# Attention and FFN mix on one core: first keys in halves, first queries in two banks, the end in two halves, and new numbers for the planner

## The chip, the cores and the metric

The kernel runs on one core of one Trainium2 chip. The metric is the device time of one execution in microseconds (us), lower is better. Before the change it is 751.2 us, the median of three runs (751.11 to 751.69).

The core has five engines that run unsynchronised, each with its own queue of instructions, all issued in the program's order: TensorE (PE) for matrix products, ScalarE (ACT), VectorE (DVE), GpSimd (POOL) and SyncE (SP, which here only issues DMAs). TensorE writes to PSUM, which has eight banks of 512 fp32 columns on 128 partitions.

## The reference

The input is 2048 rows x of 512 columns. Its output mixes a 32-head attention block (head width 16) and a SwiGLU FFN (width 1792) by a gate for each row:

```python
g = _sigmoid((x * gate_w).sum(-1, keepdims=True))
a = _A_ref(x, A_wqkv, A_wo)          # softmax(q k^T / 4) v, then @ wo
b = _B_ref(x, B_w_gate, B_w_up, B_w_down)   # (silu(x@wg) * (x@wu)) @ w_down
return g * a + (1 - g) * b
```

All tensors are bf16. The costly part is the softmax: 32 heads x 2048 x 2048 exponentials.

## The kernel before

**Tiling.** The 32 heads form 8 groups of 4; the 2048 queries form 4 blocks of 512. A *unit* is one group with one block of queries (32 units). Each unit has 16 *tiles* of 128 keys; a tile is four score banks, one for each head, of 128 keys x 512 queries. There are 512 tiles; the code counts them as slots. For each tile TensorE makes the scores (keys as weights, queries streamed, in row tiles of the array: mode "R"), an engine takes the exponential from PSUM, and TensorE multiplies the result with the values (`pv`, four matmuls in column tiles of the array: mode "C"), summing into a bank `o` for the unit. A column of ones among the values gives the softmax's denominators.

**Two ways to the exponential.** ScalarE takes most tiles, two banks at a time (1024 columns, `e_all`). VectorE takes the rest, from the last tiles of each unit: it writes scaled bits of the score as an integer (`c_t`, first one bank after another), then either three shifted copies, of which GpSimd can make some (a group of 4 terms), or two bit masks and a product (a group of 2 terms); each term is one more `pv` on TensorE.

**The planner.** Nothing of this order is fixed by loops. While the program is being written, a loop (L1986 on) keeps a model of each engine's clock (`plan.pe`, `plan.act`, `plan.dve`, `plan.pool`) and of when each bank comes free, and chooses the next thing for TensorE: a group of scores (`choose`, L874, and `emit_group`, L982), a `pv`, or a piece of side work from a list of chains with due times (`Pacer`, L50; `side`, L1880): projections of q, k and v, the FFN, output projections. `spend` (L419) charges TensorE's time: `FLIP` for a change of mode, `UNIT_US` or `PIECE_US + COLS_US` for a unit of four matmuls. `horizon` (L863) says when ScalarE will run dry by `ACT_FIX + ACT_COL` a bank, and the scores are put no later than `LATEST` ahead of that (L2004). Whether a tile goes to VectorE is decided by `wants` and `v_unit` (L1940) from VectorE's planned backlog. Some 26 weights steer the choices; `begin` (L1844) sets them anew at the slots that the table `WEIGHTS` (L160) names, some every 8 slots. So a number of the planner changes no arithmetic but can change the order of everything behind it.

**Banks.** `ordered` (L223) gives each instruction that touches a PSUM bank a wait on the last user of that bank if that was another engine, readers included. Two engines can't read one bank side by side.

**The start** (L1574 to L1612). Warm-up matmuls run while x arrives. Chunks 3 and 2 of the transposed input `xT` are made by TensorE from rows of x (`turn`) and copied out by ScalarE and VectorE; chunks 0 and 1 come by two transposing DMAs issued from SP. Then 8 matmuls give the keys of the first head group for 1024 keys (`kp0`, two banks; for each chunk in the order 3, 0, 2, 1, both banks), 4 more the queries of the first block (`qp0`, one bank). VectorE takes the largest absolute key of each row over all 1024 columns (`largest`), scales a selector by it (`k_neg`), and TensorE adds, with |q| that ScalarE made (`aq0`), a bound to the queries (`bound_add`): it keeps the exponent negative. From the bounded queries VectorE makes variant 0 (heads 0 and 2) and then, the bank being the same, ScalarE variant 1 (heads 1 and 3) of `q0a`. Then the planner's loop begins.

**The end.** The last unit's sums are made ready for division in `post` (L1426) by one ScalarE instruction over 512 queries (`osb`); `denominators` (L1482) picks out the sums, `recip16` inverts, `spread_rows` (L1486) spreads them over the partitions, four VectorE products make `on_l`, and four matmuls add the last group's share to four banks `a_ps`, which hold the output projection of the last 512 rows. The rest of that projection is 20 steps: 3 chunks `wo_t`, one `wo_l`, one that adds the FFN part, for each of four banks of 128 rows. Two banks are made as a side chain in halves of the rows (`two_banks`, L541; `last_pieces`, L1501; ten steps of two matmuls), the other two by `tail(n)` (L1517) as full-array matmuls: `tail(3)` ahead of the last two `pv` (L2055), `tail(2)` ahead of the denominators, `tail(2)` ahead of `spread_rows`, three after it.

Of the kernel before, what the change touches and what calls it, by code (L numbers as in the profile page):

```python
# [81 lines left out]
def kernel(  # L82
# [35 lines left out]
    EB = 9  # L118
    NE = 22
    NP = 8  # L120
    NY = 3
# [12 lines left out]
    HUNGRY = 0.107  # L134
    KEEP = 2
    FED = 8.063
    W3 = -1
    N1 = 6
    N2 = 0.964
    LOW = 0.782  # L140
    EXTRA = 1.717
    NEXT = 1.088
    BURST = 8.876
    SHORT = 15
    BACK = 3
    FIRST = 0.087
    W3T = 0.28
    W4 = 0.5
    W4T = 0.168
    W4B = 0.126  # L150
    LATEST = 0.64
# [3 lines left out]
    SPARE = 0.352  # L155
# [109 lines left out]
    class Ordered:  # L265
# [4 lines left out]
        def __getattr__(self, name):  # L270
            f = getattr(self.engine, name)

            def g(*a, **kw):
                out = kw["out"] if "out" in kw else a[0] if a else None
                return ordered(f(*a, **kw), [v for v in (*a, *kw.values()) if v is not out], [out])  # L275
            return g
# [129 lines left out]

    FLIP, UNIT_US, PIECE_US, COLS_US = 0.097, 0.224, 0.011, 0.213
    TO_ACT, ACT_FIX, ACT_COL, ACT_IN = 0.485, 0.064, 0.4265, 0.167
    ACT_PE, DVE_PE, PE_DVE, ACT_DVE = 0.055, 0.08, 0.24, 0.06
    GPS = 1  # L410
    OWN = 1
# [4 lines left out]
    GLEAD = 5.422  # L416
    WINDOW = 1.303

    def spend(mode, mms, ready=0.0):  # L419

        plan.seq += 1
        work_at.append((plan.pe, mms))
        plan.pe = max(plan.pe + (FLIP if mode != plan.mode else 0.0), ready) + (0.226 * mms if mode == "F" else PIECE_US + COLS_US * mms)
        plan.mode = mode
# [52 lines left out]
    def m_tile(name):  # L477
        return take(m_bank())
# [88 lines left out]
    def columns(n, name, lhs, rhs, end, c0=0):  # L567

        st = {}

        def pc(k):
            def f():
                if k == 0:
                    st["p"] = m_tile(name)
                w, r = lhs(k), rhs(k)
                for j in range(4):
                    mm(st["p"][32 * j:32 * j + 32, c0:QBW], lhsT=w[:, 32 * j:32 * j + 32], rhs=r, start=(k == 0),
                       stop=(k == n - 1), tile_position=(0, 32 * j), skip_group_check=True)
# [30 lines left out]
    def v0(t0):  # L609

        p = m_tile("vp")
        for i in range(8):
            for dc in range(DC):
                mm(p[:, 64 * i:64 * i + 64], lhsT=xT[:, dc, (t0 + i) * P:(t0 + i + 1) * P], rhs=wv[:, dc, 0:64],
                   start=(dc == 0), stop=(dc == DC - 1))
        return p
# [865 lines left out]
    def denominators(p, osb):  # L1482
        for tq in range(TQ):
            mm(p[:, 4 * tq:4 * tq + 4], lhsT=osb[:, tq * P:(tq + 1) * P], rhs=sel_t[:, :], start=True, stop=True)

    def spread_rows(p, rt):  # L1486
        for tq in range(TQ):
# [6 lines left out]
    a_ps = []  # L1494
# [6 lines left out]
    def last_pieces():  # L1501

        def keep(pa, pb):
            a_ps.extend([pa, pb])
        return two_banks(NB + 1, "a_l", last_rows(0), last_rows(1), keep, stop=False)

    rest = [(tq, i) for tq in (2, 3) for i in range(NB + 1)]

    def tail_ready():
        for c in sorted(pace.chains, key=lambda c: c.deadline):  # L1510
            force(c)
        while owed:
            pay()
        assert here_done and len(scaled) == TQ
        a_ps.append(m_tile("al"))

    def tail(n):  # L1517

        for _ in range(n):
            tq, i = rest.pop(0)  # L1520
            if tq == 3 and i == 0:
                a_ps.append(m_tile("al_o"))
            w, r = last_rows(tq)(i)
            mm(a_ps[tq][:, 0:D], lhsT=w, rhs=r, start=(i == 0), stop=False)
# [25 lines left out]
    kpart0 = const.tile([P, 3], F32, name="kpart0")  # L1550
# [41 lines left out]
    largest(0, kp0[:, :])  # L1592
    k_neg(kneg1, 0, idle[:, 0:P])
    act(out=aq0, in_=qp0[:, :], func=ACT.Abs)
    act(out=kaug[:, 0, 0:2 * QBW], in_=kp0[:, :], func=ACT.Identity, bias=onescol[:, 0:1], scale=1.0)
    vp0 = v0(0)
    bound_add(qp0, kneg1, aq0)
    vec.tensor_scalar(out=q0a[:, 0, :], in0=qp0[:, :], scalar1=vsel[:, 0:1], scalar2=None, op0=ALU.mult)
    act(out=q0a[:, 1, :], in_=qp0[:, :], func=ACT.Identity, scale=vsel[:, 1:2])
    vec.tensor_copy(out=v0_out(0), in_=vp0[:, :].rearrange("p (t h c) -> p t h c", h=4, c=DH))  # L1600
    m_free(vp0, 0.0)
    vec.tensor_copy(out=q0_bf[0], in_=qp0[:, :])
    m_free(qp0, plan.pe + 2.0)
    m_free(warm, 0.0)
# [118 lines left out]
    for pos, qb in enumerate(ORDER):  # L1723
# [13 lines left out]
        for tq in range(TQ):  # L1737
# [19 lines left out]

# [282 lines left out]
    while closed < UNITS or vops or vcur or jobs:  # L2040
# [89 lines left out]
```

## Time and profile before

One execution was profiled, 751.17 us in all; the span of its instructions is 749.4 us.

| | value |
|---|---|
| median of three runs | 751.2 us (751.11 to 751.69) |
| profiled execution | 751.17 us |
| its span, first to last instruction | 749.4 us |
| granted TensorE clock | 1.00 |
| ScalarE exponentials | 754 of 1024 columns, 4 of 1536 |
| VectorE first steps of a tile from PSUM (banks) | 528, that is 132 tiles of 512 |
| GpSimd busy | 246.2 us (33%) |
| chain that ended last, by engine | ACT 70%, PE 24%, DVE 4%, issue 2% |

In lists of groups each line names the source line, engine, operation, what is written from what, the count, then the busy time and mean ns of one, then the idle time before them and who ended it. Every operation is recorded by a helper (L260 for matmuls, L263 for ScalarE, L275 for the others), so groups are told apart by tiles. In a timeline a line begins with the start and length in us; in a table of stretches each engine has its busy time with the number of instructions in brackets. Engines work in a pipeline, so lengths of neighbours can overlap.

### The profile page before, as it was taken

To read this page: it belongs to the slowest core of one execution; us is meant where nothing else is said; L and a number is where in the kernel's file an instruction comes from. 1 tells how busy PE (TensorE), PEld (TensorE's weight loads), DVE (VectorE), ACT (ScalarE), POOL (GpSimd) and SP (SyncE) were. 2 spreads that over 40 slices of the span, in tenths; PEclk is the share of its full clock that TensorE was granted. 3 is DMA by queue.
4 is the path that set the end of the run, shared out by engine and by line. 5 is a ranking of instruction groups with operands and counts; after the bars stand their busy time and mean duration, and the time that the engine had idled before them with its cause. 6 is when DMAs were issued, how large, how long until landed. Compare 5 with 4: busy or idle time off the path is not lost.

```text
span 749.4 us, 23683 instructions
## 1 busy us (share of the span) xinstructions
PE 733.1 (98%) x10009; PEld 237.0 (32%) x10009; DVE 724.2 (97%) x1196; ACT 733.5 (98%) x827; POOL 246.2 (33%) x342
## 2 busy tenths in 40 slices
PE   7999999999999999999999999999999999999997
PEld 3333332333332333333333233233333333332332
DVE  6799999999999999999999999999999999999995
ACT  5999999999999999999999999999999999999996
POOL 5142030442534443531443322553113403403221
PEclk9999999999999999999999999999999999999999
DMA  9000212344210003220200041312000231200001
GB/s 211 23 2 16 51 32 42 72 121 101 49 36 13 20 24 82 58 53 21 59 16 11 25 109 31 70 27 60 18 23 16 62 82 42 47 19 14 14 31 36
DMA packets 91025, 34.48 MB, mean 46 GB/s; under 512 B 75488, under 2 KB 90472, under 8 KB 90920
## 3 DMA queue, kind: packets, MB, share of 16 engines
q1 hardware_dynamic: 89192, 32.66, 18.5%
q8 instruction: 78, 1.28, 0.7%
q10 hardware_dynamic: 1728, 0.33, 0.3%
q14 instruction: 27, 0.22, 0.1%
HBM read 21.55 MB, written 2.35 MB: 32 GB/s over the span
## 4 chain that ended last, share of the span: by engine, by line
ACT 70%; PE 24%; DVE 4%; issue 2%; DVEq 0%
ACT e_all L263 66%; PE psum L260 24%; ACT th L263 3%; DVE c_t L275 2%; DVE mt L275 0%; DVE gs L275 0%; DVE kaug L275 0%; ACT mt L263 0%; ACT xT L263 0%; DVE rd L275 0%; ACT osb L263 0%; DVE osb L275 0%; DVE o_t L275 0%; DVE qx L275 0%; DVE rn L275 0%
## 5 line engine op out<-in xcount | busy, mean ns | idle before, releaser
L263 ACT ACTIVATE e_all<-psum 128x1024 bf16<-128x1024 f32 x758 | 709.7, 1126 | 1.2 <-PE psum L260 1.0
L275 DVE TENSOR_SCALAR c_t<-psum 128x512 uint16<-128x512 f32 x443 | 295.4, 686 | 4.4 <-PE psum L260 3.3
L260 PE MATMUL psum<-qx,kaug 32*128 32x512 bf16 (+1 forms) x1632 | 250.3, 385 | 6.0 <-ACT e_all L263 4.4
L275 POOL TENSOR_TENSOR c_t<-c_t,lift 128x256 int32<-128x256 int32 (+2 forms) x152 | 105.7, 702 | 274.5 <-DVE c_t L275 216.3
L260 PE MATMUL psum<-e_all,vaug 128*32 128x512 bf16 (+3 forms) x2032 | 169.5, 330 | 0.0
L260 PEld LDWEIGHTS <-kaug 32*128 32x128 bf16 (+1 forms) x2048 | 76.3, 91 | 268.8 <-ACT e_all L263 195.7
L260 PEld LDWEIGHTS <-vaug 128*32 128x32 bf16 x4012 | 96.8, 95 | 125.1 <-issue 88.4
L260 PE MATMUL psum<-c_t,vaug 128*32 128x512 bf16 (+3 forms) x1712 | 132.9, 337 | 0.5 <-DVE mt L275 0.2
L275 DVE TENSOR_SCALAR c_t<-c_t 128x2048 uint16<-128x2048 uint16 (+1 forms) x191 | 129.8, 686 | 0.9
L275 POOL TENSOR_TENSOR c_t<-c_t 128x512 bf16<-128x512 bf16 (+2 forms) x54 | 49.7, 933 | 84.8 <-DVE c_t L275 45.8
L260 PE MATMUL psum<-wd_t,mt 128*32 128x512 bf16 x896 | 73.4, 382 | 0.0
L260 PE MATMUL psum<-xT,wg 128*32 128x512 bf16 x896 | 72.6, 384 | 0.0
L260 PE MATMUL psum<-xT,wu 128*32 128x512 bf16 x896 | 71.7, 383 | 0.4 <-DVE c_t L275 0.3
L275 DVE TENSOR_TENSOR c_t<-c_t 128x2048 bf16<-128x2048 bf16 (+1 forms) x42 | 50.9, 1213 | 0.0
L260 PE MATMUL psum<-q,kaug 32*128 32x512 bf16 (+1 forms) x256 | 50.1, 385 | 0.5 <-ACT e_all L263 0.2
L275 DVE TENSOR_SCALAR kaug<-psum 128x512 uint16<-128x512 f32 (+1 forms) x67 | 44.8, 687 | 0.8 <-PE psum L260 0.4
L260 PE MATMUL psum<-xT,wqk 128*32 128x512 bf16 x512 | 40.9, 383 | 0.0
L263 ACT ACTIVATE th<-psum 128x512 bf16<-128x512 f32 x56 | 38.8, 693 | 0.0
L275 DVE SCALAR_TENSOR_TENSOR gs<-th,psum 128x512 bf16<-128x512 bf16 x56 | 37.9, 676 | 0.4 <-ACT th L263 0.3
L275 DVE SCALAR_TENSOR_TENSOR mt<-gs,psum 128x512 bf16<-128x512 bf16 x56 | 37.9, 677 | 0.3
L275 POOL TENSOR_TENSOR kaug<-c_t,lift 128x256 int32<-128x256 int32 (+1 forms) x31 | 21.1, 681 | 50.3 <-DVE c_t L275 33.2
L275 POOL TENSOR_TENSOR c_t<-kaug,lift 128x256 int32<-128x256 int32 (+1 forms) x30 | 20.7, 697 | 40.1 <-DVE c_t L275 19.7
(124 smaller groups left out, 464.0 us busy)
## 6 DMA issues: line engine op xcount, KB each, us to landing
wg<-in_B_w_gate_dram SPq DMA_DIRECT2D x56, 128.0 KB
wu<-in_B_w_up_dram SPq DMA_DIRECT2D x56, 128.0 KB
on<-osb SPq DMA_DIRECT2D x120, 16.0 KB
rb<-rr SPq DMA_DIRECT2D x15, 128.0 KB
wd_t<-in_B_w_down_dram SPq DMA_DIRECT2D x7, 256.0 KB
qx<-qst SPq DMA_DIRECT2D x96, 16.0 KB
qx<-aq SPq DMA_DIRECT2D x96, 16.0 KB
out_dram<-o_t SPq DMA_DIRECT2D x12, 128.0 KB
```

The costliest lines, as they stand in the source:

```text
L260: return ordered(nc.tensor.matmul(out, lhsT=lhsT, rhs=rhs, **kw), [lhsT, rhs], [out])
L263: ordered(nc.scalar.activation(out=out, in_=in_, **kw), [in_, *kw.values()], [out])
L275: return ordered(f(*a, **kw), [v for v in (*a, *kw.values()) if v is not out], [out])
```

## The change

Four parts.

1. *First keys in halves, first queries in two banks.* The key matmuls run bank by bank, not chunk by chunk. `largest`, `k_neg` and the copy to `kaug` run for each half of 512 keys. The queries are made in two halves of 256, one in bank 4, the other in bank 7 (`warm`, which held the warm-up); |q|, the bound and the variants are made for each half, variants of one half by VectorE, of the other by ScalarE. Three of the eight value tiles go ahead of the bound, five behind.
2. *End in two halves of the queries.* `osb` is made by two ScalarE instructions of 256 queries; denominators, reciprocal, spreading and `on_l` run by halves. The 20 steps become four side chains of five steps in column tiles (mode "C"), released 8, 6, 4 and 2 slots ahead of the end; `tail(n)` takes what is left of them. `tail(3)` ahead of the last `pv` is gone; up to five steps lie between the denominators' parts and the rest ahead of the third final matmul.
3. *Planner.* Durations: `FLIP` 0.097 to 0.1055, a unit 0.224 to 0.2157, a new `TURN` of 0.0105 on entering mode "C", `ACT_FIX` 0.064 to 0.057. All first weights and nearly all entries of `WEIGHTS` are new (55 entries of 26 numbers become 54 of 27; `LATEST` is now among them). Averaged over slots 8 to 511 by the tables: the bound on the exponentials waiting for `pv` (`EB`) 9.2 to 8.6, the share of slots in which VectorE does GpSimd's kind of work itself (`OWN`) 0.86 to 0.62, `LATEST` 0.640 to 0.657.
4. The wrapper of VectorE's and GpSimd's calls records a tensor as read also where it is the output (in-place operations).

```diff
-    FLIP, UNIT_US, PIECE_US, COLS_US = 0.097, 0.224, 0.011, 0.213
-    TO_ACT, ACT_FIX, ACT_COL, ACT_IN = 0.485, 0.064, 0.4265, 0.167
+    FLIP, UNIT_US, PIECE_US, COLS_US, TURN = 0.1055, 0.2157, 0.0024, 0.2133, 0.0105
+    TO_ACT, ACT_FIX, ACT_COL, ACT_IN = 0.485, 0.057, 0.4265, 0.167
...
-        plan.pe = max(plan.pe + (FLIP if mode != plan.mode else 0.0), ready) + (0.226 * mms if mode == "F" else PIECE_US + COLS_US * mms)
+        plan.pe = max(plan.pe + (FLIP if mode != plan.mode else 0.0), ready) + (TURN if mode == "C" != plan.mode else 0.0) + (0.226 * mms if mode == "F" else PIECE_US + COLS_US * mms)
...
-            act(out=osbs[un][:, :], in_=o[:, :], func=ACT.Identity, bias=tiny[:, 0:1], scale=1.0)
+            for cs in (slice(0, QBW // 2), slice(QBW // 2, QBW)):
+                act(out=osbs[un][:, cs], in_=o[:, cs], func=ACT.Identity, bias=tiny[:, 0:1], scale=1.0)
...
-        return two_banks(NB + 1, "a_l", last_rows(0), last_rows(1), keep, stop=False)
+        return columns(NB + 1, "al", lambda i: last_rows(tq)(i)[0], lambda i: last_rows(tq)(i)[1], keep, stop=False)
...
-    for dc in arrived:
-        for tb in range(2):
+    for tb in range(2):
+        for dc in arrived:
             mm(kp0[:, tb * QBW:(tb + 1) * QBW], lhsT=wpad[1][:, dc, :], rhs=xT[:, dc, tb * QBW:(tb + 1) * QBW],
...
-    for dc in arrived:
-        mm(qp0[:, :], lhsT=wpad[0][:, dc, :], rhs=xT[:, dc, 0:QBW], start=(dc == arrived[0]), stop=(dc == arrived[-1]))
-    largest(0, kp0[:, :])
+    HW = QBW // 2
+    halves = [(qp0[:, 0:HW], slice(0, HW)), (warm[:, 0:HW], slice(HW, QBW))]
+    for p, cs in halves:
+        for dc in arrived:
+            mm(p, lhsT=wpad[0][:, dc, :], rhs=xT[:, dc, cs], start=(dc == arrived[0]), stop=(dc == arrived[-1]))
+    largest(0, kp0[:, 0:QBW])
     k_neg(kneg1, 0, idle[:, 0:P])
...
+    largest(3, kp0[:, QBW:2 * QBW])
+    k_neg(kneg1, 3, kneg1)
+    act(out=kaug[:, 0, 0:QBW], in_=kp0[:, 0:QBW], func=ACT.Identity, bias=onescol[:, 0:1], scale=1.0)
+    for p, cs in halves:
+        act(out=aq0[:, cs], in_=p, func=ACT.Abs)
+    act(out=kaug[:, 0, QBW:2 * QBW], in_=kp0[:, QBW:2 * QBW], func=ACT.Identity, bias=onescol[:, 0:1], scale=1.0)
+    vp0 = m_tile("vp")
+    v0(vp0, range(3))
+    for p, cs in halves:
+        bound_add(p, kneg1, aq0[:, cs])
+    v0(vp0, range(3, 8))
+    for v in range(2):
+        vec.tensor_scalar(out=q0a[:, v, halves[0][1]], in0=halves[0][0], scalar1=vsel[:, v:v + 1], scalar2=None, op0=ALU.mult)
+        act(out=q0a[:, v, halves[1][1]], in_=halves[1][0], func=ACT.Identity, scale=vsel[:, v:v + 1])
...
-    pace.add(last_pieces(), SLOTS - KT // 2, SLOTS, downs, cond=ripe)
+    for tq in range(TQ):
+        last.append(pace.add(last_pieces(tq), SLOTS - (KT // 2, 6, 4, 2)[tq], SLOTS + tq, downs, cond=ripe, begun=last[-1:]))
...
-        if closed == UNITS - 1 and pv_left(closed) <= 2 and not a_ps[2:]:
-            tail_ready()
-            tail(3)
         next_pv()
...
+    tail(3)
     on_l = work.tile([P, QBW], BF16, tag="rd", name="on_l")
+    rts = []
+    for h in range(2):
+        dt = m_tile("dt")
+        denominators(dt, osb, (2 * h, 2 * h + 1))
+        rts.append(work.tile([P, 4 * TQ], BF16, tag="rt", name="rt"))
+        recip16(rts[h][:, 8 * h:8 * h + 8], dt[:, 8 * h:8 * h + 8])
+    tail(1)
+    for h in range(2):
+        rps = m_tile("rps")
+        spread_rows(rps, rts[h], (2 * h, 2 * h + 1))
+        for tq in (2 * h, 2 * h + 1):
+            cs = slice(tq * P, (tq + 1) * P)
+            vec.tensor_tensor(out=on_l[:, cs], in0=osb[:, cs], in1=rps[:, cs], op=ALU.mult)
+    tail(1)
+    while len(a_ps) < 2:
+        tail(1)
     for tq in range(TQ):
+        if tq == 2:
+            tail(TQ * (NB + 1))
         mm(a_ps[tq][:, 0:D], lhsT=on_l[:, tq * P:(tq + 1) * P], rhs=wo_l[:, 1, :], start=False, stop=True,
```

More of the change, by code (lines that the diff above doesn't have):

```diff
@@ L117 @@
     UNIT = [(qb, 0) for qb in range(QB)] + [(qb, g) for qb in range(QB) for g in range(1, G)]
-    EB = 9
+    EB = 10
     NE = 22
@@ L133 @@
     D_US = (0.0, 0.6, 1.133)
-    HUNGRY = 0.107
+    HUNGRY = 0.208
     KEEP = 2
-    FED = 8.063
-    W3 = -1
+    FED = 7.822
+    W3 = -0.842
     N1 = 6
[L139 to L142, printed above, removed]
+    N2 = 2.473
+    LOW = 1.544
+    EXTRA = 1.184
+    NEXT = 1.047
     BURST = 8.876
[L144 to L151, printed above, removed]
+    SHORT = 12
+    BACK = 2
+    FIRST = 0.245
+    W3T = -0.164
+    W4 = 4
+    W4T = 0.255
+    W4B = 0.186
+    LATEST = 0.599
     TINY = 1e-37
@@ L274, in g @@
                 out = kw["out"] if "out" in kw else a[0] if a else None
-                return ordered(f(*a, **kw), [v for v in (*a, *kw.values()) if v is not out], [out])
+                reads = [*a["out" not in kw:], *(v for k, v in kw.items() if k != "out")]
+                return ordered(f(*a, **kw), reads, [out])
             return g
@@ L405 @@
     held = [None] * NP
-    FLIP, UNIT_US, PIECE_US, COLS_US = 0.097, 0.224, 0.011, 0.213
-    TO_ACT, ACT_FIX, ACT_COL, ACT_IN = 0.485, 0.064, 0.4265, 0.167
+    FLIP, UNIT_US, PIECE_US, COLS_US, TURN = 0.1055, 0.2157, 0.0024, 0.2133, 0.0105
+    TO_ACT, ACT_FIX, ACT_COL, ACT_IN = 0.485, 0.057, 0.4265, 0.167
     ACT_PE, DVE_PE, PE_DVE, ACT_DVE = 0.055, 0.08, 0.24, 0.06
     GPS = 1
-    OWN = 1
+    OWN = 0
     POOL_IN, POOL_FIX, POOL_ONE, POOL_PE, POOL_OVER = 0.12, 0.12, 0.43, 0.2, 0.1
@@ L415 @@
     TAKE_C = 1
-    GLEAD = 5.422
-    WINDOW = 1.303
+    GLEAD = 5.764
+    WINDOW = 1.503
     def spend(mode, mms, ready=0.0):
@@ L565, in two_banks, with columns @@
         return [(1, pc(k), 2 if k == 0 else 0, "R", st if k == n else None) for k in range(2 * n)]
-    def columns(n, name, lhs, rhs, end, c0=0):
+    def columns(n, name, lhs, rhs, end, c0=0, stop=True):
         st = {}
@@ L577, in f @@
                     mm(st["p"][32 * j:32 * j + 32, c0:QBW], lhsT=w[:, 32 * j:32 * j + 32], rhs=r, start=(k == 0),
-                       stop=(k == n - 1), tile_position=(0, 32 * j), skip_group_check=True)
+                       stop=(stop and k == n - 1), tile_position=(0, 32 * j), skip_group_check=True)
                 spend("C", 1)
@@ L607, in k_bound, with v0 @@
         vec.tensor_reduce(out=kb[:, b:b + 1], in_=kst[b][:, :], axis=AX.X, op=ALU.max, apply_absolute_value=True)
-    def v0(t0):
-        p = m_tile("vp")
-        for i in range(8):
+    def v0(p, tiles):
+        for i in tiles:
             for dc in range(DC):
-                mm(p[:, 64 * i:64 * i + 64], lhsT=xT[:, dc, (t0 + i) * P:(t0 + i + 1) * P], rhs=wv[:, dc, 0:64],
+                mm(p[:, 64 * i:64 * i + 64], lhsT=xT[:, dc, i * P:(i + 1) * P], rhs=wv[:, dc, 0:64],
                    start=(dc == 0), stop=(dc == DC - 1))
-        return p
     def v0_out(t0):
@@ L1480, in recip, with denominators, spread_rows @@
             at.setdefault(n0 + 13 + b, []).append(lambda norm=norm: later(0.345, norm, fast=True))
-    def denominators(p, osb):
-        for tq in range(TQ):
+    def denominators(p, osb, tqs=range(TQ)):
+        for tq in tqs:
             mm(p[:, 4 * tq:4 * tq + 4], lhsT=osb[:, tq * P:(tq + 1) * P], rhs=sel_t[:, :], start=True, stop=True)
-    def spread_rows(p, rt):
-        for tq in range(TQ):
+    def spread_rows(p, rt, tqs=range(TQ)):
+        for tq in tqs:
             for j in range(4):
@@ L1493 @@
     here_done = []
-    a_ps = []
+    a_ps = {}
     def last_rows(t):
@@ L1499, in last_rows, with last_pieces, keep @@
                           (osbs[UNITS - 2][:, cs], wo_l[:, 0, :]) if i == NB - 1 else (ident[:, :], bblk[:, t, :]))
-    def last_pieces():
-        def keep(pa, pb):
-            a_ps.extend([pa, pb])
-        return two_banks(NB + 1, "a_l", last_rows(0), last_rows(1), keep, stop=False)
[L1507 to L1515, printed above, removed]
+    def last_pieces(tq):
+        def keep(p):
+            a_ps[tq] = p
+        return columns(NB + 1, "al", lambda i: last_rows(tq)(i)[0], lambda i: last_rows(tq)(i)[1], keep, stop=False)
+    last = []
     def tail(n):
         for _ in range(n):
[L1520 to L1524, printed above, removed]
+            c = next((c for c in last if not c.out()), None)
+            if c is None:
+                return
+            while not ripe():
+                if owed:
+                    pay()
+                else:
+                    for f in at.pop(min(at)):
+                        f()
+            emit_piece(c)
     def out_pieces(qb, tq):
@@ L1548, in keep_warm @@
             mm(warm[:, :], lhsT=idle[:, 0:P], rhs=idle[:, :], start=True, stop=True)
-    kpart0 = const.tile([P, 3], F32, name="kpart0")
+    kpart0 = const.tile([P, 4], F32, name="kpart0")
     kneg0 = mt[:, 3, P:2 * P]
@@ L1594 @@
[L1594 to L1599, printed above, removed]
-    vec.tensor_copy(out=v0_out(0), in_=vp0[:, :].rearrange("p (t h c) -> p t h c", h=4, c=DH))
-    m_free(vp0, 0.0)
@@ L1602 @@
-    vec.tensor_copy(out=q0_bf[0], in_=qp0[:, :])
-    m_free(qp0, plan.pe + 2.0)
-    m_free(warm, 0.0)
+    HW = QBW // 2
[4 more added lines that the diff above has]
+    largest(0, kp0[:, 0:QBW])
+    k_neg(kneg1, 0, idle[:, 0:P])
+    largest(3, kp0[:, QBW:2 * QBW])
+    k_neg(kneg1, 3, kneg1)
@@ L1605 @@
+    vec.tensor_copy(out=v0_out(0), in_=vp0[:, :].rearrange("p (t h c) -> p t h c", h=4, c=DH))
+    for p, cs in halves:
+        vec.tensor_copy(out=q0_bf[0][:, cs], in_=p)
+    m_free(vp0, plan.pe + 1.0)
+    m_free(qp0, plan.pe + 1.6)
+    m_free(warm, plan.pe + 2.0)
     for g in (3, 4):
@@ L1844, in begin @@
     def begin(n):
-        nonlocal HUNGRY, KEEP, FED, W3, W3T, W4, W4T, W4B, N1, N2, LOW, EXTRA, NEXT, SPARE, BURST, SHORT, BACK, FIRST, EB, OWN, NY, TAKE_C, TAKE_P, GLEAD, WINDOW, FACE
+        nonlocal HUNGRY, KEEP, FED, W3, W3T, W4, W4T, W4B, N1, N2, LOW, EXTRA, NEXT, SPARE, BURST, SHORT, BACK, FIRST, EB, OWN, NY, TAKE_C, TAKE_P, GLEAD, WINDOW, FACE, LATEST
         plan.slot = n
         if n in WEIGHTS:
-            HUNGRY, KEEP, FED, W3, W3T, W4, W4T, W4B, N1, N2, LOW, EXTRA, NEXT, SPARE, BURST, SHORT, BACK, FIRST, EB, OWN, NY, TAKE_C, TAKE_P, GLEAD, WINDOW, FACE = WEIGHTS[n]
+            HUNGRY, KEEP, FED, W3, W3T, W4, W4T, W4B, N1, N2, LOW, EXTRA, NEXT, SPARE, BURST, SHORT, BACK, FIRST, EB, OWN, NY, TAKE_C, TAKE_P, GLEAD, WINDOW, FACE, LATEST = WEIGHTS[n]
         for c in need.get(n, []):
@@ L2006 @@
             n_pv = pv_list(plan.pe)
-            switch = 0.0 if plan.mode == "C" else FLIP
+            switch = 0.0 if plan.mode == "C" else FLIP + TURN
             fits = int((room + SLACK - switch) / UNIT_US)
@@ L2053 @@
             continue
-        if closed == UNITS - 1 and pv_left(closed) <= 2 and not a_ps[2:]:
-            tail_ready()
-            tail(3)
         next_pv()
     for c in sorted(pace.chains, key=lambda c: c.deadline):
-        force(c)
+        if c not in last:
+            force(c)
     while owed:
@@ L2072 @@
     osb = osbs[un]
-    tail(2)
-    dt = m_tile("dt")
-    denominators(dt, osb)
-    rt = work.tile([P, 4 * TQ], BF16, tag="rt", name="rt")
-    recip16(rt[:, :], dt[:, 0:4 * TQ])
-    tail(2)
-    rps = m_tile("rps")
-    spread_rows(rps, rt)
-    tail(len(rest))
-    on_l = work.tile([P, QBW], BF16, tag="rd", name="on_l")
+    tail(3)
+    on_l = work.tile([P, QBW], BF16, tag="rd", name="on_l")
+    rts = []
[14 more added lines that the diff above has]
+        tail(1)
     for tq in range(TQ):
-        cs = slice(tq * P, (tq + 1) * P)
-        vec.tensor_tensor(out=on_l[:, cs], in0=osb[:, cs], in1=rps[:, cs], op=ALU.mult)
-    for tq in range(TQ):
+        if tq == 2:
+            tail(TQ * (NB + 1))
         mm(a_ps[tq][:, 0:D], lhsT=on_l[:, tq * P:(tq + 1) * P], rhs=wo_l[:, 1, :], start=False, stop=True,
-           skip_group_check=tq < 2)
+           skip_group_check=True)
     for tq in range(TQ):
```

4 lines of the change are left out of this document (2 added, 2 removed).

## The prediction

> **What bounds the kernel now.** I read the page's busy times first, then a table of stretches, then the timeline of the start and of the end, and last the starts of ScalarE's instructions one by one. The page and the stretches:
>
> ```profile
> PE 733.1 (98%) x10009; PEld 237.0 (32%) x10009; DVE 724.2 (97%) x1196; ACT 733.5 (98%) x827; POOL 246.2 (33%) x342
> ```
>
> ```profile
> 0.00:13.44 13.44, 10.71 (x79) 5.22 (x80) 7.88 (x31) 5.48 (x9) 10.71 (x28) 1.00 0.98 172
> 13.44:40.00 26.56, 25.27 (x310) 7.99 (x313) 21.67 (x42) 26.11 (x30) 4.29 (x7) 1.00 0.26 78
> 40.00:735.00 695.00, 687.09 (x9526) 220.46 (x9523) 687.46 (x1110) 694.35 (x783) 229.96 (x305) 1.00 0.18 43
> 735.00:741.00 6.00, 6.00 (x65) 2.09 (x62) 4.66 (x8) 5.59 (x6) 1.22 (x2) 1.00 0.01 3
> ```
>
> Busy times stand in the order PE, PEld, DVE, ACT, POOL. From 40 to 735 us ScalarE is idle 0.65 us, TensorE 7.9, VectorE 7.5; GpSimd has two thirds free. ScalarE holds the middle, the other two have one per cent left. The time is then three parts: a start until the exponentials flow (13.44 us), the flow, and the end after the last exponential (740.65 to 749.4 us).
>
> "Busy" hides something. From the start of one 1024-column exponential to the next the trace has 904 ns at the least, 905 in the middle, 921 in the mean of 694 pairs after 14 us; each lasts 1.02 to 1.13 us, so a wait below some 0.1 to 0.2 us shows as no idle time. Together the pairs lie 639.0 - 694 x 0.904 = 11.6 us above their floor: ScalarE waits a little for scores, often. The Trainium skill, page "Perfetto Trace Analysis", section "Identifying the Most-Contended Engine", calls occupancy a fair measure of the distance to the limit for Vector, Scalar and GPSIMD. By that rule the middle could win 0.65 us from ScalarE's idle time and no more; the starts above contradict it, and the rule gives the rival "edges only" below.
>
> The start:
>
> ```profile
> 7.93 2.75 PE L260 MATMUL psum<-xT,mt 128*128 128x512 bf16 x12 [0.45 <-ACT xT L263]
> ...
> 9.86 1.23 DVE L275 TENSOR_REDUCE kpart<-psum 128x1 f32<-128x1024 f32 x1 [1.49 <-PE psum L260]
> ...
> 11.12 0.35 DVE L275 SCALAR_TENSOR_TENSOR mt<-mt,kpart 128x128 bf16<-128x128 bf16 x1
> ...
> 11.62 0.40 PE L260 MATMUL psum<-mt 128*32 128x512 bf16 x4
> ...
> 12.06 0.75 DVE L275 TENSOR_SCALAR mt<-psum,vsel 128x512 bf16<-128x512 f32 x1 [0.59 <-PE psum L260]
> ```
>
> Keys, maximum, selector, bound, variant 0: one chain. Scores follow at 12.87, the first exponential at 13.44. ScalarE's variant 1 waits for VectorE's 0 (same bank), to 13.54, and its scores come at 13.59.
>
> The end:
>
> ```profile
> 740.44 0.82 PE L260 MATMUL psum<-wo_t,on 128*128 128x512 bf16 x3
> ...
> 741.19 0.62 PE L260 MATMUL psum<-e_all,vaug 128*32 128x512 bf16 x8
> ...
> 741.86 0.69 ACT L263 ACTIVATE osb<-psum,tiny 128x512 bf16<-128x512 f32 x1 [1.21 <-PE psum L260]
> ...
> 742.89 0.26 DVE L275 RECIPROCAL rt<-psum 128x16 bf16<-128x16 f32 x1 [3.20 <-PE psum L260]
> ...
> 743.77 0.88 DVE L275 TENSOR_TENSOR on_l<-osb,psum 128x128 bf16<-128x128 bf16 x4 [0.62 <-PE psum L260]
> ...
> 744.65 1.41 DVE L275 TENSOR_SCALAR mt<-psum,gval 128x512 bf16<-128x512 f32 x2
> ```
>
> The last exponential ends at 740.65, but TensorE is in `tail(3)` until its next start at 741.19: the last two `pv` come about 0.45 us late.
>
> **Part 1, the start.** Half the keys need four matmuls, at 0.216 from start to start and 0.38 for the last (rows of the twelve): 7.93 + 0.65 + 0.38 = 8.96, against 9.82 for all eight. But the order 3, 0, 2, 1 now wants chunk 0 at 8.15 and chunk 1 at 8.58, and the trace has the last part of the two transposing DMAs landing at 8.26 and 8.87 (before, they were first used at 8.36 and 9.23, behind nothing). So TensorE waits for chunk 1: the fourth matmul starts at 8.91, first half done 9.29. Queued behind that wait are the second half (done 10.15) and the queries (four halves at 0.11, done about 10.6 and 11.0); VectorE waits for them. VectorE: a maximum over 512 takes 0.65 (mean of the two later ones, 654 ns), so 9.33 to 9.98, selector 0.35 to 10.37, second maximum to 11.06, second selector to 11.44. Before: 11.47. Splitting wins 0.53 in front and pays 0.48 in the second round: a net of 0.03. The second bank wins the rest. The bound for 256 columns takes 0.28 (277 ns, the 256-column form): from 11.59, both halves by 11.98. Variant 0 of half one on VectorE: 1024 columns cost 1.21 and 512 0.68 from PSUM, 1.04 ns a column, so 0.75 - 0.27 = 0.48: done 12.39; of half two on ScalarE: 1.11 against 0.69 for 1024 and 512, 0.82 ns a column, 0.48: 12.02 to 12.50. Scores at 12.53 against 12.87: **-0.35**. Variant 1 follows near 12.88 against 13.54. ScalarE's extra instructions (one more copy to `kaug`, one more |q|) lie in its 2.5 us wait for `qp0`; without that cover each costs its fixed part, 0.11. Bounds: 0 (a later landing, or the |q| halves late) to -0.6.
>
> Then ScalarE idled 0.39 ahead of its third exponential (15.76), where TensorE did 24 matmuls of side work first. Variant 1 now comes 0.66 earlier, and the first weights are others: half of it, **-0.2**, bounds -0.4 and +0.4. Moving five value tiles behind the bound puts 20 matmuls at 0.029, 0.6 us, between bound and scores, from 11.75 to 12.35: hidden until 12.53, and 0.18 is what remains of that cover.
>
> **Part 2, the end.** Without `tail(3)` the last `pv` pair can start at 740.75: -0.45. `osb` in halves: 0.48 each, overlapping by 0.11, so 741.17 to 742.02 where one instruction would end at 741.86: the second half is 0.16 later. Behind it: two denominators 0.2, reciprocal 0.26, eight spreading matmuls 0.3, two products 0.48, the last matmul 0.38, ScalarE's eviction 0.69, with five hand-overs of 0.04 to 0.08: 744.6. VectorE's second eviction, behind four products and the first, ends at 744.85 against 746.06. That is -1.2, the 0.45 included, if nothing of the 20 steps is left over. The steps cost the same in either form: a row-half pair, a column step and a full step each start 0.216 after the other. 13 ran ahead of the last `pv` before; five now lie behind it, so 15 must fit ahead of it, and TensorE has no idle time there (6.00 of 6.00): two steps more, +0.43, either ahead or in the rest that the third final matmul waits for. Column steps share the `pv`'s mode: entering and leaving the full-array form cost 0.31 against 0.216 twice, 0.19, which is inside the -0.45. **-0.7**; bounds -1.3 (all fit) and +1.0 (ten steps, 2.16 us, left over).
>
> **Part 3, the planner.** The trace bears out the new durations: units of a run start 0.216 apart, the first after a change of mode takes 0.226, score to `pv` and `pv` to score 0.321, that is 0.105 more. The old ones charge 0.642 for scores with one `pv` and 0.866 with two, the new ones 0.653 and 0.869: errors near 0.01 that cancel. ScalarE's pair was planned at 0.917 and is now at 0.910, against 0.921 that ran. If the flow followed, 754 x 0.007 = 5.3 us would go. But each tile that leaves ScalarE (two exponentials, 1.81 us) costs VectorE 4 x 0.68 + 2 x 0.69 = 4.1 and TensorE two to three units, 0.65. VectorE's 7.5 us of idle time hold one such tile whole, not two (8.2). I take one tile and a little of the waiting: **-2.0**. No row shows what the new weights do. Gain at most: the 11.6 us of waits. Loss: a lower `EB` and less `OWN` can leave VectorE idle and send tiles back at 1.81 each, three for +5.4. The value sits nearest to the idle-time rows. Hidden by nothing: ScalarE has no cover, so whatever it takes more is seen in full.
>
> Part 4 adds recorded reads on the same engine, which runs in order: 0; if a POOL or ACT partner gained a wait, it would show in the bounds of part 3.
>
> Sum: -0.35 - 0.2 - 0.7 - 2.0 = -3.25 on the profiled execution's 751.17 us (span 749.4, and 1.8 around it, unchanged). It lies at the median of 751.2. Forecast **747.9 us**.
>
> **Rivals.** *Edges only*: the flow keeps its tiles and its pitch, 749.9 (-1.25). For: ScalarE's row is 99.9% full. Against: the 11.6 us. *The flow tightens*: pitch 0.914 in the mean, -5.3, and the edges: 744.7. For: scores planned at the true pace, `LATEST` higher on average, so scores earlier. Against: only 1% of idle time beside ScalarE. *Slower*: VectorE takes fewer tiles. Its place is `wants` and `own_now`: with `OWN` off in 38% of the slots its gaps stay empty, with a lower `EB` TensorE must turn to `pv` sooner. Each tile back costs 1.81; from one tile on the edges are eaten (+0.6), with two 753.5. Against: VectorE's gaps were 1% in any case. *The start doesn't do what it says*: chunk 1 lands later than 8.87, by 0.35 or more, and the halves win nothing; 748.2, inside the forecast's range.
>
> **How the numbers follow.** A measurement here tells 0.2%, 1.5 us, from no change. Forecast with its start variant 0.47, flow tightens 0.22, edges only 0.18, slower 0.13. The forecast's own range is 746.3 to 749.6. Faster: 0.47 + 0.22 + under half of edges only (0.07) = 0.76; same 0.11; slower 0.13. The range reaches from the tightened flow to one to two tiles back: 744.6 to 752.4.
>
> **What would show it.** Scores near 12.5 and the first exponential near 13.1; a wait of TensorE for a DMA between 8.6 and 8.9; under 1516 banks in ScalarE's exponentials (1520 now); mean start to start under 0.921; last `pv` within 0.1 of the last exponential's end; last exponential to end 8.0 instead of 8.75. Wrong it would be if ScalarE's share of tiles grew, or if a block of projection steps stood ahead of the third final matmul.

## The result and the profile after

The changed kernel takes 753.13 us (median of 13 runs, 752.7 to 754.2) against 751.19 us before (13 runs, 750.7 to 751.71): a ratio of 1.0026, 95% interval 1.0018 to 1.0035. It is slower by 1.9 us where the prediction said 3.2 us faster, and it lies above the stated range of 744.6 to 752.4. The profiled execution took 752.92 us, its span is 751.2.

First the page's busy times after, then the stretches (PE, PEld, DVE, ACT, POOL busy), over the same times as before:

```profile
PE 731.4 (97%) x10143; PEld 236.6 (31%) x10143; DVE 714.9 (95%) x1186; ACT 737.2 (98%) x828; POOL 259.1 (34%) x367
```

```profile
0.00:13.44 13.44, 11.48 (x97) 5.81 (x101) 8.67 (x35) 6.65 (x12) 10.71 (x28) 1.00 0.96 174
40.00:735.00 695.00, 683.39 (x9570) 218.64 (x9574) 676.22 (x1095) 693.93 (x777) 244.07 (x332) 1.00 0.18 43
735.00:741.00 6.00, 5.79 (x91) 2.07 (x83) 5.74 (x8) 6.00 (x6) 0.00 (x0) 1.00 0.01 3
```

ScalarE did 3.7 us more in all, VectorE 9.3 us less. From 40 to 735 us VectorE now stands idle for 18.8 us (7.5 before), while ScalarE is nearly as full as it was (1.07 us idle, 0.65 before). Work moved the wrong way. The groups of ScalarE's exponentials tell how much, before first, then after:

```profile
L263 ACT ACTIVATE e_all<-psum 128x1024 bf16<-128x1024 f32 x754 | 704.7, 1124 | 1.2 <-PE psum L260 1.0
...
L263 ACT ACTIVATE e_all<-psum 128x1536 bf16<-128x1536 f32 x4 | 5.8, 1470 | 0.0
```

```profile
L263 ACT ACTIVATE e_all<-psum 128x1024 bf16<-128x1024 f32 x737 | 695.3, 1148 | 1.8 <-PE psum L260 1.7
...
L263 ACT ACTIVATE e_all<-psum 128x1536 bf16<-128x1536 f32 x18 | 28.8, 1612 | 0.0
```

That is 2 x 754 + 3 x 4 = 1520 banks before and 2 x 737 + 3 x 18 = 1528 after. Eight banks are two tiles: 130 on VectorE instead of 132.

The start, in the timeline:

```profile
7.69 3.17 PE L260 MATMUL psum<-xT,mt 128*128 128x512 bf16 x16 [0.45 <-ACT xT L263]
7.69 0.10 PEld L260 LDWEIGHTS <-mt 128*128 128x128 bf16 x1 [0.73 <-issue]
8.15 0.31 PEld L260 LDWEIGHTS <-mt 128*128 128x128 bf16 x2 [0.37 <-issue]
8.75 1.83 PEld L260 LDWEIGHTS <-mt 128*128 128x128 bf16 x12 [0.28 <-issue]
...
9.16 0.69 DVE L276 TENSOR_REDUCE kpart<-psum 128x1 f32<-128x512 f32 x1 [1.03 <-PE psum L260]
...
11.37 0.40 PE L260 MATMUL psum<-mt 128*32 128x256 bf16 x8 [0.16 <-ACT mt L263]
...
11.71 0.87 DVE L276 TENSOR_SCALAR mt<-psum,vsel 128x256 bf16<-128x256 f32 x2 [0.49 <-PE psum L260]
11.82 0.84 ACT L263 ACTIVATE mt<-psum,vsel 128x256 bf16<-128x256 f32 x2
...
12.83 7.44 ACT L263 ACTIVATE e_all<-psum 128x1024 bf16<-128x1024 f32 x8 [0.17 <-PE psum L260]
```

VectorE and ScalarE now make the variants side by side (11.71 and 11.82), and the exponentials run on from 12.83 without the pause that stood ahead of the third. The first key matmul starts at 7.69 here and at 7.93 before; in the runs below it lies anywhere from 7.5 to 8.4, as the input lands. So lengths are counted from it: to the first exponential 5.14 us (5.51 before), to the third 6.96 (7.83 before). One thing this does not take out: TensorE now needs chunks 0 and 1 of the input sooner. They landed at 8.11 and 8.70, the second key matmul (weights loaded at 8.15) starts 0.25 us later than the usual distance of 0.216, the fourth (8.75) 0.16 later. So 5.14 holds 0.41 us of waiting for the input; 5.51 holds none.

The end, in the timeline:

```profile
743.52 0.39 PE L260 MATMUL psum<-e_all,vaug 128*32 128x512 bf16 x4
...
743.96 0.84 ACT L263 ACTIVATE osb<-psum,tiny 128x256 bf16<-128x256 f32 x2 [0.51 <-PE psum L260]
...
745.62 0.88 DVE L276 TENSOR_TENSOR on_l<-osb,psum 128x128 bf16<-128x128 bf16 x4 [0.32 <-PE psum L260]
745.97 0.69 PEld L260 LDWEIGHTS <-on_l 128*128 128x128 bf16 x4 [0.49 <-DVE on_l L276]
745.97 1.04 PE L260 MATMUL psum<-wo_l,on_l 128*128 128x512 bf16 x4 [0.32 <-DVE on_l L276]
746.42 1.40 DVE L276 TENSOR_SCALAR mt<-psum,gval 128x512 bf16<-128x512 f32 x2
```

The last exponential ends at 743.46 and the last `pv` starts 0.06 later. The four final matmuls follow each other with no projection step between them. From the last exponential to the end it is 7.74 us (8.80 before).

What lies between is the flow. From the start of the third exponential to the end of the last, one stretch of each kernel, before first, then after:

```profile
15.76:740.64 724.88, 715.83 (x9861) 229.58 (x9855) 711.92 (x1156) 724.11 (x814) 235.47 (x314) 1.00 0.18 43
```

```profile
14.65:743.46 728.81, 715.63 (x9992) 229.18 (x9987) 702.57 (x1142) 727.19 (x812) 248.35 (x339) 1.00 0.18 43
```

The flow grew by 3.93 us, the edges shrank by 0.87 and 1.06. The difference, 2.0, is the measured loss (1.9 between the medians). From one 1024-column exponential to the next the mean is 921 ns in both kernels, and both lie 11.6 to 11.7 us above the floor of 904 in sum. So it is not the pace that changed but the number: 8 banks at 0.452 (904 ns for two) are 3.62 of the 3.93 us.

### The profile page after: what moved, and what is told of

The parts are those of the page before. It is cut to its first block, busy times and chain, and to the rows that moved or that the text cites. A ratio compares the mean times of both kernels' runs of the same rounds, so it can differ in the third digit from the quotient of the medians.

```text
span 751.2 us, 23975 instructions
## 1 busy us (share of the span) xinstructions
PE 731.4 (97%) x10143; PEld 236.6 (31%) x10143; DVE 714.9 (95%) x1186; ACT 737.2 (98%) x828; POOL 259.1 (34%) x367
## 4 chain that ended last, share of the span: by engine, by line
ACT 71%; PE 15%; DVE 10%; issue 2%; DMA 2%; SPq 0%; DVEq 0%
ACT e_all L263 67%; PE psum L260 15%; DVE c_t L276 6%; ACT th L263 3%; DMA xT<-in_A_x_dram 1%; DVE kaug L276 1%; DMA wg<-in_B_w_gate_dram 1%; DVE osb L276 0%; DVE wd_t L276 0%; DVE qst L276 0%; DVE o_t L276 0%; ACT mt L263 0%; DVE gs L276 0%; DMA out_dram<-o_t 0%; DMA on<-osb 0%
## 5 line engine op out<-in xcount | busy, mean ns | idle before, releaser
L263 ACT ACTIVATE e_all<-psum 128x1024 bf16<-128x1024 f32 (+1 forms) x755 | 714.8, 1159 | 1.8 <-PE psum L260 1.7
L276 DVE TENSOR_SCALAR c_t<-psum 128x512 uint16<-128x512 f32 x467 | 310.2, 683 | 11.1 <-PE psum L260 9.3
L276 POOL TENSOR_TENSOR c_t<-c_t,lift 128x256 int32<-128x256 int32 (+1 forms) x177 | 121.7, 695 | 196.5 <-DVE c_t L276 158.1
L260 PE MATMUL psum<-c_t,vaug 128*32 128x512 bf16 (+3 forms) x1736 | 130.2, 331 | 0.9 <-DVE c_t L276 0.8
L276 DVE TENSOR_SCALAR c_t<-c_t 128x2048 uint16<-128x2048 uint16 (+1 forms) x184 | 125.0, 688 | 1.3
L276 POOL TENSOR_TENSOR c_t<-c_t 128x256 bf16<-128x256 bf16 (+2 forms) x73 | 65.7, 910 | 134.5 <-DVE c_t L276 84.7
L276 POOL TENSOR_TENSOR kaug<-c_t,lift 128x256 int32<-128x256 int32 (+1 forms) x48 | 32.0, 675 | 86.2 <-DVE c_t L276 65.8
L276 DVE TENSOR_TENSOR c_t<-c_t 128x2048 bf16<-128x2048 bf16 (+1 forms) x35 | 42.3, 1210 | 0.0
L260 PEld LDWEIGHTS <-mt 128*32 128x32 bf16 (+1 forms) x1045 | 22.5, 95 | 29.4 <-issue 24.5
L276 DVE TENSOR_SCALAR kaug<-psum 128x512 uint16<-128x512 f32 x44 | 29.2, 683 | 0.7 <-PE psum L260 0.7
```

Source lines behind the costliest of these rows:

```text
L260: return ordered(nc.tensor.matmul(out, lhsT=lhsT, rhs=rhs, **kw), [lhsT, rhs], [out])
L263: ordered(nc.scalar.activation(out=out, in_=in_, **kw), [in_, *kw.values()], [out])
L276: return ordered(f(*a, **kw), reads, [out])
```

## The experiments

All are compared with the kernel before on the same chip. From chip to chip its median lies between 750.9 and 751.2 us.

**The edges on the order of before.** In four kernels the planner's state is kept as it was, so that it writes the same flow as before; only what lies around it is changed. In their traces ScalarE, VectorE and GpSimd have the same instructions in the same order between the start and the end, and the flow from the third exponential to the last takes 724.9 us in each, as before.

`e1_start`, the new start alone. The second half of the queries goes to bank 3, since the old order takes bank 7 at once:

```diff
-    halves = [(qp0[:, 0:HW], slice(0, HW)), (warm[:, 0:HW], slice(HW, QBW))]
+    halves = [(qp0[:, 0:HW], slice(0, HW)), (psum[:, 3, 0:HW], slice(HW, QBW))]
```

> The kernel before, its planner and order of work untouched, with the new start alone (second query half in bank 3). Theory (the edges win, the flow loses by two tiles that went back to ScalarE): the first exponential starts 5.1 us after the first key matmul instead of 5.5, and the flow behind it is only moved: 750.5 us, and 750.2 if the pause of 0.39 us ahead of the third exponential goes too; ScalarE keeps 1520 banks. Rival (the start wins nothing, chunk 1 of the input lands too late): 751.2.

`e6_tail3`, one move at the end:

```diff
             tail_ready()
-            tail(3)
...
-    tail(2)
+    tail(3)
     dt = m_tile("dt")
```

> The kernel before with one edit: the three projection steps ahead of the last two pv go behind them. Theory: the last pv come 0.45 us earlier and the end with them, 750.7. Rival (the steps are only moved and are paid behind): 751.2.

`e2_end`, the end by halves, the four banks' steps in their old forms, and `e3_start_end`, both edges:

> The kernel before with the new end alone: osb in halves, denominators, spreading and products by halves, tail(3) behind the last pv; the four rows' steps stay as they were (two banks in row halves, two as full matmuls), so that the planner decides as before. Theory: last exponential to the end 7.8 us instead of 8.75: 750.2. Rival (halves pay their fixed parts and the steps left over hold up the third final matmul): 751.2 or more.

> Both edges on the order of work of before. Theory: the gains add, 749.5 us, ratio to before 0.998; against the changed kernel's 753.1 the difference is then the flow alone, 3.6 us = two tiles of 1.81. Rival (the edges are worth nothing or cost time in the changed kernel): 751.2 or more.

| kernel | us | ratio to before, 95% | first key matmul to 1st / 3rd exponential | last exponential to end |
|---|---|---|---|---|
| e1_start | 750.89 | 0.9997, 0.9988 to 1.0006 | 4.87 / 7.58 | 8.81 |
| e6_tail3 | 750.67 | 0.9994, 0.9985 to 1.0003 | 5.50 / 7.82 | 8.51 |
| e2_end | 750.24 | 0.9992, 0.9983 to 1.0000 | 5.50 / 7.82 | 8.13 |
| e3_start_end | 750.21 | 0.9988, 0.9979 to 0.9997 | 4.72 / 7.43 | 8.14 |

The end is worth 0.67 us in the profile, 0.3 to 0.4 of it by the move of `tail(3)`. The times forecast for `e2_end` and `e6_tail3` came out (750.2 and 750.7), though the length from the last exponential to the end is 8.13 where 7.8 was expected; "only moved" is refuted by the profiles, while both intervals still reach 1. The start was a miss, and with it the sum: `e1_start` was expected at 750.5 and `e3_start_end` at 749.5. In `e1_start` the first exponential came 0.64 us earlier, the third only 0.25. The timeline of `e3_start_end` shows where it went:

```profile
12.86 0.40 PE L260 MATMUL psum<-xT,mt 128*32 128x512 bf16 x4
12.94 0.74 DVE L276 CAST mt<-psum 128x256 bf16<-128x256 f32 x2
...
13.74 1.26 PE L260 MATMUL psum<-xT,mt 128*32 128x512 bf16 x20 [0.48 <-DVE mt L276]
...
15.36 1.94 ACT L263 ACTIVATE e_all<-psum 128x1024 bf16<-128x1024 f32 x2 [0.77 <-PE psum L260]
```

The old order gives bank 3 to side work at once. TensorE stops 0.48 us for VectorE's copy of the query half out of that bank, and the scores of the third exponential are queued behind it. It is my choice of bank, not the change's.

`e7_copies_first` puts both copies ahead of the value tiles, bank 3 first:

```diff
-    vec.tensor_copy(out=v0_out(0), in_=vp0[:, :].rearrange("p (t h c) -> p t h c", h=4, c=DH))
-    for p, cs in halves:
+    for p, cs in halves[::-1]:
         vec.tensor_copy(out=q0_bf[0][:, cs], in_=p)
+    vec.tensor_copy(out=v0_out(0), in_=vp0[:, :].rearrange("p (t h c) -> p t h c", h=4, c=DH))
```

> Both edges on the order of work of before, but VectorE copies the two query halves out of their banks (bank 3 first) ahead of the value tiles. In the run without that, TensorE waited 0.48 us at 13.7 us for bank 3, which the order of before gives to side work at once, and the third exponential started 7.4 us after the first key matmul. Theory (a bank taken early eats the start's gain): the wait goes, the third exponential starts 7.0 us after the first key matmul, 749.8 us. Rival (the 24 side matmuls alone set it): no change, 750.2.

It took 749.60 us (749.27 to 750.01), ratio 0.9981, 0.9972 to 0.9990: faster than both kernels. In its timeline the 24 side matmuls run through and the first three exponentials stand in one row:

```profile
12.47 0.75 DVE L276 CAST mt<-psum 128x256 bf16<-128x256 f32 x2
12.60 3.07 ACT L263 ACTIVATE e_all<-psum 128x1024 bf16<-128x1024 f32 x3 [0.17 <-PE psum L260]
...
12.81 1.48 PE L260 MATMUL psum<-xT,mt 128*32 128x512 bf16 x24
```

First key matmul to third exponential is 7.13 us, and the flow behind it is that of before (724.88 there):

```profile
14.65:739.57 724.92, 715.98 (x9866) 229.59 (x9861) 712.75 (x1157) 724.15 (x814) 235.51 (x314) 1.00 0.18 43
```

So the two edges win 1.3 us on the old flow (0.70 at the start and 0.67 at the end in the profile), and the changed kernel, whose edges are another 0.56 better, loses all of that and 1.9 more in its flow.

**Which half of the start wins.** `e4_queries` keeps the keys' loop and the one maximum of 1024 and halves the queries alone; `e5_keys` does the reverse. Both leave all eight value tiles ahead of the bound.

> The kernel before with the queries' halves alone (keys as before, in one maximum of 1024; copies of the queries ahead of the values). Theory, from the prediction: the halves of the queries win 0.35 us from first key matmul to first exponential (5.51 to 5.2), nearly all of the start's gain. Rival: the keys' halves win it, 5.5 here.

> The kernel before with the keys' halves alone (queries in one bank). Theory, from the prediction: first key matmul to first exponential 5.5 us, a gain of 0.03. Rival (the first maximum and ScalarE's first copy run sooner and win it): 5.2.

First key matmul to first exponential: 5.14 us with the queries alone, 5.48 with the keys alone, 5.51 before. Both numbers are the theories', but the second not for the theory's reason. With the keys alone the second selector is ready 3.17 us after the first key matmul instead of 3.54; the bound still starts at 3.66 (3.68 before), because TensorE first works through the 32 matmuls of the value tiles. In `e3_start_end`, where both halves are in, five value tiles stand behind the bound and TensorE never waits for the input, the selector is ready at 3.13, the bound starts at 3.27 and the first exponential at 4.72. So the queries' two banks win 0.37 by themselves, and the keys' halves some 0.4 more once the value tiles are out of the way. In the changed kernel that second part is lost: its selector is ready at 3.54, as before, after the 0.41 us of waiting for the input. In `e1_start` this wait is 0.15, the difference between its 4.87 and 4.72. (`e4_queries` and `e5_keys` ran once each, 751.09 and 751.17 us: the totals also hold when the input landed, 0.5 us apart.)

**The planner's numbers, taken apart.** Five kernels undo or do one part of the planner's change.

`f2_planner`: before, with the new durations, first weights and table. `f1_durations`: before, with the new durations alone. `f3_old_planner`: after, with the old planner. `f4_actfix`: after, with one number back:

```diff
-    TO_ACT, ACT_FIX, ACT_COL, ACT_IN = 0.485, 0.057, 0.4265, 0.167
+    TO_ACT, ACT_FIX, ACT_COL, ACT_IN = 0.485, 0.064, 0.4265, 0.167
```

`f5_own`: after, with `OWN` at 1 in the first weights and in every entry of the table.

> The kernel before with the planner's part of the change alone (durations, first weights, table), old start and old end. The order of work that the planner then writes has 128 tiles on VectorE (132 before, 130 in the changed kernel). Theory (the time of the flow is ScalarE's bank count, 1.81 us a tile): 4 x 1.81 = 7.2 slower than before, 758.3. Rival (the new numbers make a better flow, the edges are what costs): under 751.2.

> The kernel before with the durations of the planner alone (TensorE's four and ScalarE's 0.057), weights, start and end as before (and the recorded in-place reads). 126 tiles on VectorE instead of 132. Theory (the table of weights is fitted to one exact course of the planner, and the time is the tile count): 751.1 + 6 x 1.81 = 762.0. Rival (durations nearer the chip's make a better flow whatever the weights): 751 or less.

> The changed kernel with the planner's durations, first weights and table of before: only the new start and the new side chains of the end differ from before. 125 tiles on VectorE. Theory (the old weights fit the old start and no other): 753.1 + 5 x 1.81 = 762.2, though each part of it is as in a faster kernel. Rival (the new weights are what costs the changed kernel its time): 749.5.

> The changed kernel with one constant back: ScalarE's fixed part 0.064 instead of 0.057. 126 tiles on VectorE. Theory: 753.1 + 4 x 1.81 = 760.4. Rival (0.057 alone made the planner leave tiles on ScalarE, and 0.064 gives them back): 749.5.

> The changed kernel with VectorE allowed to do GpSimd's kind of work in all slots (OWN 1 throughout). 126 tiles on VectorE. Theory: 753.1 + 4 x 1.81 = 760.4, whatever VectorE's idle time. Rival, from the prediction (OWN off is what leaves VectorE empty): VectorE's idle time falls and the time with it, under 753.

| kernel | tiles on VectorE | banks on ScalarE | us (two runs each) | ratio to before, 95% |
|---|---|---|---|---|
| f2_planner | 128 | 1536 | 761.25 | 1.0138, 1.0120 to 1.0157 |
| f5_own | 126 | 1544 | 763.82 | 1.0171, 1.0141 to 1.0201 |
| f4_actfix | 126 | 1544 | 764.00 | 1.0173, 1.0144 to 1.0203 |
| f3_old_planner | 125 | 1548 | 770.22 | 1.0256, 1.0226 to 1.0286 |
| f1_durations | 126 | 1544 | 772.56 | 1.0287, 1.0258 to 1.0317 |

Every rival fell: no single part, done or undone, gives a flow near the old one. The theory's sign held each time, its size was 3 to 11 us short. In these kernels the exponentials also wait more: the sum above the floor of 904 ns is 13.1 to 19.5 us (11.6 before). In `f1_durations`, the farthest off, the end grew as well, from 8.80 to 11.96 us after the last exponential: projection steps now stand ahead of the last `pv`. The stretch of the flow of `f5_own` shows VectorE's idle time:

```profile
14.45:754.18 739.73, 720.65 (x9932) 229.44 (x9928) 693.26 (x1111) 735.90 (x825) 220.39 (x308) 1.00 0.18 42
```

With `OWN` on throughout VectorE is idle for 739.7 - 693.3 = 46 us, more than the 26 of the changed kernel in its own flow: switching `OWN` on does not fill VectorE. What `OWN` does by itself can't be read from this, since the whole order differs. The reading that fits all five is that the table of weights belongs to one exact course of the planner: a change of 7 ns in one constant, or a new start, sends it down another course, for which its later entries were not chosen. That the course changes is shown by the tile counts; that the entries were chosen for the old course is inferred.

**What a tile costs by itself.** Since the upset flows cost more than 1.81 us a tile, two more kernels take tiles away from `e7_copies_first` late, with the order up to there untouched:

```diff
         plan.slot = n
+        if n == 464:
+            ACT_FIX = 0.057
         if n in WEIGHTS:
```

(376 instead of 464 in `g2_tile130`.)

> The order of work of before with both edges and copies first (749.6 us, 132 tiles on VectorE), up to slot 464 of 512 instruction by instruction the same; from there ScalarE's fixed part in the planner is 0.057 instead of 0.064, and the order it writes has 131 tiles on VectorE. Theory (a tile that goes back costs ScalarE's two exponentials, 4 banks of 0.452): 749.6 + 1.8 = 751.4. Rival (as in the kernels where the whole flow was upset, each tile brings as much again in new waits): 752.5 or more.

> The same with the switch at slot 376: 130 tiles on VectorE, as many as in the changed kernel, from the order of before. Theory: 749.6 + 3.6 = 753.2, the changed kernel's time by its tile count. Rival (new waits, or other properties of the changed kernel's flow): 755 or more, or near 751.

`g1_tile131`: 751.89 us (751.35 to 752.97, ratio to before 1.0013, 1.0004 to 1.0021), 2.3 above its base for one tile, between theory and rival. In its profile the flow grew by 2.05 us (726.97 against 724.92), a tile's 1.81 and a little; the base ran on another chip, on which the kernel before is 0.13 us faster. `g2_tile130`: 753.10 us (752.97 to 753.60, ratio 1.0028, 1.0017 to 1.0038), 3.5 above for two. The groups of `g2_tile130`:

```profile
L263 ACT ACTIVATE e_all<-psum 128x1024 bf16<-128x1024 f32 x752 | 703.2, 1130 | 1.0 <-PE psum L260 0.7
...
L263 ACT ACTIVATE e_all<-psum 128x1536 bf16<-128x1536 f32 x8 | 11.8, 1486 | 0.0
```

1528 banks, as in the changed kernel, and its flow takes 728.48 us from the third exponential, against 728.81 in the changed kernel and 724.92 without the switch. The same tile count by another road gives the same flow. With that the loss is settled as two tiles; why the changed planner leaves these two to ScalarE is not shown.

## Why the prediction was wrong

**The start: right.** -0.35 was forecast from bank to bank; the first exponential came 0.37 earlier. The account holds too: the keys' halves were to win a net of 0.03 because TensorE would wait 0.33 us for chunk 1. It waited 0.25 for chunk 0, which was not foreseen, and 0.16 for chunk 1; the selector came 3.54 us after the first key matmul in both kernels, and all of the gain is the second bank's. That `e5_keys` gave 0.03 too is luck: there the value tiles held the bound. The pause ahead of the third exponential was put at half, -0.2; all of it went, -0.50 (from first to third 1.82 instead of 2.32).

**The end: right, under-sized.** -0.7 forecast, -1.06 measured. The 0.45 for `tail(3)` came out at 0.3 in the profile of `e6_tail3` and 0.40 in its median. The fear of left-over steps was wrong for the changed kernel: the side chains had all but four of the 20 steps done ahead of the last `pv`, and those four fit behind it, so the +0.43 fell away.

**The planner: wrong, and its term decides the sign.** The step that failed is "VectorE's 7.5 us of idle time hold one such tile whole ... I take one tile and a little of the waiting: -2.0". It reads room on an engine as work that will be put there. In place of it the flow grew by 3.93 us, and the prediction's own sign against it came true, 1528 banks on ScalarE instead of under 1516: VectorE got two tiles fewer and its idle time from the third exponential to the last rose from 13.0 to 26.2 us (724.88 - 711.92, 728.81 - 702.57). Room was there before and was not used after. What fills it is a rule of choice with a backlog, buffers and due times, and the profile of before holds nothing of what other weights do to that rule. The bound of that term, three tiles back for +5.4, held the result; the value chosen had the wrong sign. Nor can the loss be laid on the new numbers alone. With the old numbers the new start and side chains leave VectorE 125 tiles and take 770.2 us (`f3_old_planner`), so under this start the new numbers win 17 us; they don't win back all that the old start and the old numbers had together.

**The pace.** The new durations are the chip's: 0.226, 0.216 and 0.321 us are found again in the changed kernel's starts. But the planner's price for ScalarE's pair went from 0.917 to 0.910, away from the 0.921 that runs in both kernels and towards the floor of 0.904. Over 755 exponentials that makes any flow 5.3 us shorter in the planner's own clock and none on the chip, so that a flow with 3.6 us more of ScalarE's work can look shorter there. This is worked out, not shown: `f4_actfix` puts the price back, and with it the whole order changes (764.0 us). One reading was off without harm: an exponential lasts 1.02 to 1.33 us in the trace of before, 1.13 is only the middle; the 11.6 us above the floor come from the starts.

**The rivals.** "Slower" was the true one, with its number: two tiles back, 753.5 forecast, 753.13 measured; that it fits so well is in part luck, as the edges won 0.7 more and the flow lost 0.3 more than its sum has. Its place, `OWN` and `EB`, is open: `OWN` on throughout gave no tiles back in `f5_own`, in an order that differs everywhere, and `EB` alone was not tried. "Edges only" and "the flow tightens" fell. Part 4 was put at 0, and `e1_start` and `e3_start_end`, which have it, keep the flow of before. The Trainium skill, page "Perfetto Trace Analysis", section "Identifying the Most-Contended Engine", calls ScalarE's occupancy a fair measure of how near the limit it is. The 11.6 us of short waits below the busy row said otherwise, and they are real; yet they stayed at 11.7, and the time followed ScalarE's amount of work as the page's rule would have it. I gave "the flow tightens" more than this row could carry.

## What to carry to other kernels

A kernel whose order is written by a planner with fitted weights can hardly be changed at one place: an edit that touches the planner's state re-orders all behind it, so first hold the order fixed and measure the edit by itself. When an engine is full, count its instructions before and after; here the bank count told the changed kernel's result, and it fell short by 3 to 11 us only where the whole order was upset. Idle time on the other engines is room, not gain, until one sees what would fill it. And a part that wins nothing alone can win beside another: look at what holds the next step in each run before adding up gains.

## What was not expected of the hardware

The first key matmul starts between 7.5 and 8.4 us in the profiles of kernels whose beginning is the same, as the rows of x land sooner or later; half a microsecond between two profiles' totals at the start means nothing by itself. And an instruction that starts on time hides its waits: successive exponentials lie mostly 904 or 920 ns apart, and those whose scores arrive less than 60 ns ahead, over half of them, hold about 10 of the 11.6 us above the floor, with no idle time shown on ScalarE.
